# Windowed attention into a squared-ReLU FFN: spare slots and earlier visits for late pairs, and a last accumulator in two tiles

## The chip, the cores and the metric

The kernel runs on one core of a Trainium2 chip, in one launch. The metric is the device time of an execution in microseconds (us). The core's engines are TensorE (PE, matrix products), VectorE (DVE), ScalarE (ACT), GpSimd (POOL) and SyncE (SP, which here issues nearly all DMAs).

## The reference

Attention with 4 batches, 8 heads, 768 positions and a head dimension of 64. Each query sees the keys less than 16 positions away and, beside them, one summary for each of the 24 blocks of 32 positions (the largest of the block's keys by element, and the mean of its values). The result, 3072 tokens of 512 numbers, goes through a feed-forward network with 2048 hidden units and a squared ReLU.

```python
k_sum = k.reshape(B, H, nb, block, D).max(axis=3)
v_sum = v.reshape(B, H, nb, block, D).mean(axis=3)
scores_l_m = np.where(mask_l, scale * q @ k.T, -1e9)        # |i - j| < 16
scores_s = scale * np.einsum('bhsd,bhnd->bhsn', q, k_sum) + np.log(block)
a = softmax(np.concatenate([scores_l_m, scores_s], axis=-1))
x = (a @ np.concatenate([v, v_sum], axis=2)).reshape(3072, 512)
h = x @ w_in                  # 512 -> 2048
r = np.maximum(h, 0.0)
return (r * r) @ w_out        # 2048 -> 512
```

(The lines are shortened; the types are all 32-bit floats.)

## The kernel before, in words

**Numbers.** The feed-forward products are made of 32-bit floats that are split into a high and a low part, so that one product is three matmuls of 128x512 (high by high, high by low, low by high). An operand's high part is a cast on ACT (`gh`, L1810), its low part a subtraction on DVE (`gl`, L1815).

**Tiles.** The 3072 queries are 48 groups of 64, two of them a pair (24 pairs); eight groups (512 tokens) are a unit of the network, u = 0 to 5. Units 0 and 1 go through the network plainly. Units 2 to 5 go in two rounds, s = 0 (units 2 and 3) and s = 1 (units 4 and 5), each as two units by two halves of the network with seven block products instead of eight. The first products (`first_product`, L1492: `h` from `xh`, `xl` and a weight) make the hidden values; the second ones (`products`, L1738) are 56 chunks of six matmuls a round, numbered n = 0 to 55, into accumulators in PSUM of 128x1024 (`o_66`, `o_67`; each covers two banks, one for each half of 512 columns). `products(s, 0)` has the first 16 chunks, `products(s, 1)` the other 40. `copied` (ACT) and `plus` (DVE) bring an accumulator into SBUF or add it to what lies there, `leave` stores a finished block.

**Visits.** The attention of the later pairs is woven into the products. A visit on PE consists of the score matmuls of a pair n (Sn: `att` from keys `kb` and queries `q`, L734) and the value matmuls of an earlier pair v (Vv: `x` from the weights `a` and the values `v`, L1013); the table VISITS says which go together, and `visit_at` when each is due. Between the two lies `pair_softmax` (L890): DVE and ACT make the weights, DVE transposes them (L973), SP stores the transposed rows to memory (`turn`, L985, four DMAs) and fetches them back in another layout (`a`, L992, two DMAs of 384 and 128 KB). All pairs share one tile `a_81` for these rows, so that the fetch for one pair can start only when the value matmuls of the pair before have read theirs. Queries have two slots (`q`, loaded at L650), value rows three (`v_77` to `v_79`, one for each group, loaded at L671), weight chunks eight (loaded at L1794). `vps` (L606) are the matmuls of the block means of the last batch.

**Order.** A list scheduler, `Plan`, writes every engine's instructions in order before the launch. A task has an engine, an assumed cost, a key (when it is due), the tasks it comes after and the slots it takes and frees; of the tasks that are ready on an engine the one with the lowest key goes first. For a DMA the planner assumes a rate, a latency and what the argument `late` adds. On the chip each engine follows its list, and waits by semaphores where data or a slot are not there; SP too issues its DMAs in the list's order.

**The end.** The last chunk (n = 55 of s = 1) is emitted in two halves by columns, each of three matmuls. Both halves lie in one accumulator tile. The first half is copied by ACT (`copied`, L1752), the second by DVE (L1844), into two halves of one SBUF tile, and each is stored by a DMA (L1763).

## Time and profile before

| | us |
|---|---|
| median of three runs | 590.36 |
| lowest, highest | 589.26, 592.49 |
| the profiled execution | 593.21 |
| its span | 591.5 |
| PE busy in the span | 577.7 (98%) |
| PE load busy (weights, beside PE) | 469.1 (79%) |
| DVE busy | 413.6 (70%) |
| ACT busy | 353.7 (60%) |
| POOL busy | 69.5 (12%) |
| mean rate of the DMAs | 268 GB/s |

The span is the time from the first to the last instruction of the profiled execution; its own device time is 1.7 us longer. All starts below count from the span's beginning. The busy share of an engine is an average over the whole span; where the share is below one, the views by stretch tell where. The trace's visits can be told by their tiles: `att<-kb,q` are the scores, `x<-a,v` the values.

### The profile page before, as it was taken

The page shows a single profiled execution, that of the slowest core. Times are in us where ns is not written, and L with a number is a line of the kernel's source. Part 1 is how long each engine was busy: PE and PEld are TensorE (multiplying, and loading weights), DVE is VectorE, ACT ScalarE, POOL GpSimd, SP SyncE. Part 2 cuts the span into 40 slices and gives each one's busy share as a digit, 9 for nine tenths or more (in the row PEclk, how much of TensorE's full clock was granted, in tenths as well). Part 3 has the DMA queues.
Part 4 walks back from the last instruction along what each step waited for, and adds up shares of the span by engine and source line. Part 5 has one row for each costly group of instructions (what it writes and reads, how often), then busy time and mean ns, then how long its engine had stood idle before and what let it go on. Part 6 is the DMA issues. An engine that isn't in the chain of part 4 may idle for free.

```text
span 591.5 us, 12509 instructions
## 1 busy us (share of the span) xinstructions
PE 577.7 (98%) x4624; PEld 469.1 (79%) x4624; DVE 413.6 (70%) x652; ACT 353.7 (60%) x801; POOL 69.5 (12%) x116
## 2 busy tenths in 40 slices
PE   7989999999999999999999999999999999999996
PEld 6677887878888788878887788788887888788885
DVE  4899997864455578375877887689936533897653
ACT  1799876874663446456664556555556766755542
POOL 4500002214542820100000000000000000000000
PEclk9999999999999999999999999999999999999999
DMA  8996994689999759999999986988799785567672
GB/s 298 361 368 226 343 325 141 199 247 368 359 324 322 239 168 326 307 285 299 353 326 280 329 265 195 312 241 252 226 342 315 257 268 161 146 193 230 195 229 94
DMA packets 98474, 158.41 MB, mean 268 GB/s; under 512 B 9839, under 2 KB 54639, under 8 KB 98414
## 3 DMA queue, kind: packets, MB, share of 16 engines
q1 hardware_dynamic: 98030, 157.03, 81.7%
q8 instruction: 37, 0.61, 0.4%
q0 software_dynamic: 384, 0.59, 0.3%
q14 instruction: 23, 0.19, 0.1%
HBM read 112.16 MB, written 45.88 MB: 267 GB/s over the span
## 4 chain that ended last, share of the span: by engine, by line
PE 72%; DMA 11%; DVE 8%; SPq 3%; issue 2%; ACT 2%; DVEq 0%; ACTq 0%
PE o L1826 25%; PE h L1512 13%; PE o L1663 12%; PE o L1234 9%; PE h L1210 8%; PE x L1013 3%; DMA raw<-wW 3%; PE att L734 2%; DMA a<-turn 2%; DMA out<-os 2%; DMA v<-vF 1%; DVE w L1163 1%; DVE t L1155 1%; DMA fv_lent<-vS 1%; DVE raw L1149 1%
## 5 line engine op out<-in xcount | busy, mean ns | idle before, releaser
L1826 PE MATMUL o<-gh,w 128*128 128x512 f32 x448 | 121.1, 392 | 0.0
L1810 ACT CAST gh<-g 128x512 fp32r<-128x512 f32 x112 | 69.2, 621 | 56.0 <-PE o L1826 31.5
L1826 PEld LDWEIGHTS o<-gh,w 128*128 128x128 f32 x448 | 83.4, 188 | 18.0 <-issue 0.4
L1815 DVE TENSOR_TENSOR gl<-g,gh 128x512 fp32r<-128x512 f32 x112 | 75.5, 686 | 21.2 <-ACT gh L1810 21.0
L1210 PE MATMUL h<-xh,w 128*128 128x512 f32 x240 | 74.8, 393 | 0.1
L1512 PE MATMUL h<-xh,w 128*128 128x512 f32 x224 | 69.9, 393 | 0.2 <-DVE xl L1100 0.2
L1826 PE MATMUL o<-gl,w 128*128 128x512 f32 x224 | 69.2, 389 | 0.0
L1234 PE MATMUL o<-w,gh 128*128 128x512 f32 x240 | 61.9, 393 | 0.5 <-DVE w L1163 0.5
L935 ACT ACTIVATE p<-p,nm 128x88 f32<-128x88 f32 x120 | 42.7, 358 | 23.6 <-DVE nm L929 23.6
L1234 PEld LDWEIGHTS o<-w,gh 128*128 128x128 f32 x240 | 44.5, 188 | 10.6 <-DVE w L1163 0.9
L1210 PEld LDWEIGHTS h<-xh,w 128*128 128x128 f32 x240 | 44.6, 188 | 10.1 <-DVE xl L1100 0.6
L1512 PEld LDWEIGHTS h<-xh,w 128*128 128x128 f32 x224 | 41.6, 188 | 9.5 <-DVE xl L1100 0.6
L1826 PEld LDWEIGHTS o<-gl,w 128*128 128x128 f32 x224 | 42.0, 188 | 8.8
L1210 PE MATMUL h<-xl,w 128*128 128x512 f32 x120 | 46.7, 389 | 0.0
L1512 PE MATMUL h<-xl,w 128*128 128x512 f32 x112 | 43.6, 389 | 0.0
L1522 ACT ACTIVATE r<-h 128x512 f32<-128x512 f32 x32 | 19.1, 595 | 39.1 <-PE h L1512 36.0
L1224 DVE TENSOR_TENSOR gl<-r,gh 128x512 fp32r<-128x512 f32 x30 | 24.6, 823 | 15.0 <-ACT gh L1221 13.9
L1663 PE MATMUL o<-w,w 128*128 128x512 f32 x140 | 34.5, 390 | 0.0
L1234 PE MATMUL o<-w,gl 128*128 128x512 f32 x120 | 33.6, 389 | 0.0
L1803 DVE TENSOR_TENSOR g<-g 128x512 f32<-128x512 f32 x48 | 32.7, 687 | 1.0
L1219 ACT ACTIVATE r<-h 128x512 f32<-128x512 f32 x30 | 17.7, 591 | 23.5 <-PE h L1210 15.6
L1663 PEld LDWEIGHTS o<-w,w 128*128 128x128 f32 x140 | 26.2, 188 | 5.9 <-DVE u L1695 0.5
(198 smaller groups left out, 993.9 us busy)
## 6 DMA issues: line engine op xcount, KB each, us to landing
raw<-wW SPq DMA_DIRECT2D x32, 512.0 KB, 6.6
w<-scr_s SPq DMA_DIRECT2D x64, 256.0 KB, 3.0
w<-scr_a SPq DMA_DIRECT2D x48, 256.0 KB, 3.0
w<-scr_i SPq DMA_DIRECT2D x38, 256.0 KB, 5.1
scr_t<-ci SPq DMA_DIRECT2D x16, 512.0 KB, 5.4
turn<-ta SPq DMA_DIRECT2D x80, 96.0 KB, 3.8
a<-turn SPq DMA_DIRECT2D x20, 384.0 KB, 5.2
w<-scr_t SPq DMA_DIRECT2D x28, 256.0 KB, 3.6
```

The lines of the kernel that those rows point to most:

```text
L935: nc.scalar.activation(x, x, AF.Exp, bias=nm.tile[:, n : n + 1], accum_out=nm.tile[:, H + n : H + n + 1])
L1013: nc.tensor.matmul(x_of(i)[h % 2 * D : (h % 2 + 1) * D, h // 2, :], lhsT=v_bufs[g].tile[:rows, h * D : (h + 1) * D], rhs=av[:rows, 2 * c : ...
L1210: nc.tensor.matmul(cut(h), lhsT=lhs.tile[:, k * P : (k + 1) * P], rhs=rhs[:, k, c0 : c0 + n], start=(i == 0), stop=(i == 3 * KT - 1),)
L1224: lambda: nc.vector.tensor_tensor(out=cut(gl), in0=cut(r), in1=cut(gh).bitcast(F32), op=ALU.subtract),
L1234: nc.tensor.matmul(o_of(o, t), lhsT=terms[i][0].tile[:, (t - t0) * P : (t - t0 + 1) * P], rhs=terms[i][1].tile, start=(first and i == 0), ...
L1512: nc.tensor.matmul(h.tile, lhsT=lhs.tile[:, k * P : (k + 1) * P], rhs=rhs[:, k, c0 : c0 + TU], start=(i == 0), stop=(i == 3 * KT - 1),)
L1522: t2 = add(f"RL{name}", "ACT", 0.56, lambda: nc.scalar.activation(r.tile, h.tile, AF.Relu), due + 3, [t1], take=[r], use=[h])
L1663: nc.tensor.matmul(o.tile[:, bank], lhsT=chunk.tile[:, w * HALF + d * P : w * HALF + (d + 1) * P], rhs=xs[y][d], start=starts and i == 0, ...
L1803: lambda x=x, ins=ins, op=op: nc.vector.tensor_tensor(out=x.tile, in0=ins[0].tile, in1=ins[1].tile, op=op),
L1810: f"GH{s}_{n}", "ACT", 0.54, lambda x=x, gh=gh: nc.scalar.copy(out=gh.tile, in_=x.tile), due - 4, ready,
L1815: lambda x=x, gh=gh, gl=gl: nc.vector.tensor_tensor(out=gl.tile, in0=x.tile, in1=gh.tile.bitcast(F32), op=ALU.subtract),
L1826: nc.tensor.matmul(o.tile[:, d], lhsT=chunk.tile[:, w * HALF + d * P : w * HALF + (d + 1) * P], rhs=y.tile, start=begins and w == 0 and y ...
```

## The change

It has three parts. (1) Two pairs, 20 and 22, get their rows `a` in slots of the pool `t` (three tiles of 128x1024 which the second products use otherwise) and no more in the one tile `a_81`; and the planner assumes 2.5 us more for the fetch of `a` for pairs 12 and later (`late=TR_LATE`, in the planner only). (2) Seven visits (those with V17 to V23) are given earlier due times, by 8, 10 or 16 of the planner's us. (3) The accumulator that the last round's chunks of the first, third, fifth and seventh product share is two PSUM tiles of one bank each from the pool `h`, in place of one tile of two banks. `copied` and `plus` do two operations on it, one for each half; at the end DVE copies the first half and ACT the second, each into an SBUF tile of its own with a store of its own.

```diff
+SPARE_A = 20, 22
+TR_LATE = 2.5
+SOONER = {17: 8.0, 18: 8.0, 19: 10.0, 20: 16.0, 21: 16.0, 22: 16.0, 23: 16.0}
...
-        visit_at.append(at)
+        visit_at.append(at - SOONER.get(v, 0.0))
...
-                a_bufs[g] = buf("a", 1, (P, 2 * DM), F32, f"a{g}", fixed=True)
+                if g // 2 in SPARE_A:
+                    a_bufs[g] = buf("t", 3, (P, 2 * DM), F32, f"a{g}")
+                else:
+                    a_bufs[g] = buf("a", 1, (P, 2 * DM), F32, f"a{g}", fixed=True)
...
-        t_a = add(f"TR{g}", "SP", 0.8, fetch, fetch_at, [t_w], take=[a], use=[d], size=8 * P * DM, behind=last_of("turn", None))
+        t_a = add(f"TR{g}", "SP", 0.8, fetch, fetch_at, [t_w], take=[a], use=[d], size=8 * P * DM, behind=last_of("turn", None), late=TR_LATE if both[0] >= NW * 2 else 0.0)
...
+        if s == NS - 1:
+            if part == 0:
+                made["ends"] = tuple(h_buf(f"end{d}") for d in range(2))
+            acc[0] = made["ends"]
...
+        def halves(to, o):
+            if isinstance(o, tuple):
+                return [(by_two(to)[:, d], x.tile, d) for d, x in enumerate(o)]
+            return [(by_two(to), o.tile, slice(0, 2))]
...
+            def copy():
+                for x, y, _ in halves(to, o):
+                    nc.scalar.copy(out=x, in_=y)
...
+            def plus_():
+                for y, z, d in halves(to, o):
+                    nc.vector.tensor_tensor(out=y, in0=z, in1=by_two(x)[:, d], op=ALU.add)
...
-                            o.tile[:, d], lhsT=chunk.tile[:, w * HALF + d * P : w * HALF + (d + 1) * P], rhs=y.tile,
+                            o[d].tile if isinstance(o, tuple) else o.tile[:, d],
+                            lhsT=chunk.tile[:, w * HALF + d * P : w * HALF + (d + 1) * P], rhs=y.tile,
...
-                            t = copied("C21", tail, o, due + 2, [t_p], [tail], d)
-                        leave(f"21_{s}_{i}", tail, 1, 0, due + 3, [t], d)
+                        tail = buf("t", 3, (P, 2 * DM), F32, f"c21_{s}_{i}")
+                        copy = nc.scalar.copy if i else nc.vector.tensor_copy
+                        t = made["C21"] = add(
+                            f"C21_{s}_{i}", "ACT" if i else "DVE", 0.62, lambda copy=copy, x=o[i], to=tail: copy(out=to.tile[:, :TU], in_=x.tile),
+                            due + 2, [t_p], take=[tail], use=[o[i]],
+                        )
+                        rows = rest_out[HALF + i * P : HALF + (i + 1) * P, s * 2 * TU : s * 2 * TU + TU]
+                        add(
+                            f"PS21_{s}_{i}", "SP", 0.45, lambda rows=rows, tail=tail: nc.sync.dma_start(out=rows, in_=tail.tile[:, :TU]),
+                            due + 3, [t], use=[tail], size=4 * P * TU,
+                        )
```

How the lists move is seen best at three places. The first is on PE at S20 (the `att` rows; `gh_13` and `gl_13` are the operands of chunk n = 13). Before:

```order
680 L1826 MATMUL o_67<-gh_13_3756,w_986 128x512 x4
681 L1826 MATMUL o_67<-gl_13_3759,w_986 128x512 x2
682 L734 MATMUL att<-kb,q_3728 32x128 x16
683 L734 MATMUL att<-kb,q_3731 32x128 x16
684 L1826 MATMUL o_67<-gh_14_3768,w_868 128x512 x4
685 L1826 MATMUL o_67<-gl_14_3777,w_868 128x512 x2
686 L606 MATMUL vps_3835<-fv_0_3459,means 24x128 x8
687 L606 MATMUL vps_3835<-fv_2_3578,means 24x128 x8
688 L606 MATMUL vps_3835<-fv_4_3594,means 24x128 x8
689 L1826 MATMUL o_67<-gh_15_3779,w_868 128x512 x4
```

The same rows of the changed kernel:

```order
680 L1850 MATMUL o_67<-gh_13_3753,w_986 128x512 x4
681 L1850 MATMUL o_67<-gl_13_3758,w_986 128x512 x2
682 L1850 MATMUL o_67<-gh_14_3766,w_868 128x512 x4
683 L1850 MATMUL o_67<-gl_14_3769,w_868 128x512 x2
684 L740 MATMUL att<-kb,q_3739 32x128 x16
685 L740 MATMUL att<-kb,q_3742 32x128 x16
686 L612 MATMUL vps_3826<-fv_0_3459,means 24x128 x8
687 L612 MATMUL vps_3826<-fv_2_3578,means 24x128 x8
688 L612 MATMUL vps_3826<-fv_4_3594,means 24x128 x8
689 L1850 MATMUL o_67<-gh_15_3778,w_868 128x512 x4
```

S20 has gone one chunk back, behind n = 14, and `vps` follows it directly, where n = 14 stood between the two. Ahead of this place S19 with V15 has moved one chunk back too, from behind nine chunks to behind ten.

The second is on PE at V20 (`x<-a,v`). Before:

```order
833 L1826 MATMUL o_66<-gh_16_4459,w_932 128x512 x4
834 L1826 MATMUL o_66<-gl_16_4465,w_932 128x512 x2
835 L1826 MATMUL o_66<-gh_17_4469,w_932 128x512 x4
836 L1826 MATMUL o_66<-gl_17_4474,w_932 128x512 x2
837 L1826 MATMUL o_66<-gh_18_4472,w_986 128x512 x4
838 L1826 MATMUL o_66<-gl_18_4476,w_986 128x512 x2
839 L1826 MATMUL o_66<-gh_19_4504,w_986 128x512 x4
840 L1826 MATMUL o_66<-gl_19_4507,w_986 128x512 x2
841 L1013 MATMUL x_4524<-a_81,v_79 64x64 x8
842 L1013 MATMUL x_4524<-a_81,v_77 64x64 x8
843 L1826 MATMUL o_66<-gh_20_4510,w_868 128x512 x4
844 L1826 MATMUL o_66<-gl_20_4522,w_868 128x512 x2
```

In the changed kernel, at the same rows:

```order
833 L1850 MATMUL o_66<-gh_16_4461,w_932 128x512 x4
834 L1850 MATMUL o_66<-gl_16_4467,w_932 128x512 x2
835 L1019 MATMUL x_4492<-a_4346,v_79 64x64 x8
836 L1019 MATMUL x_4492<-a_4346,v_77 64x64 x8
```

V20 stands here behind n = 16. The rows that follow it, to V21:

```order
837 L1850 MATMUL o_66<-gh_17_4471,w_932 128x512 x4
838 L1850 MATMUL o_66<-gl_17_4474,w_932 128x512 x2
839 L1850 MATMUL o_66<-gh_18_4479,w_986 128x512 x4
840 L1850 MATMUL o_66<-gl_18_4489,w_986 128x512 x2
841 L1850 MATMUL o_66<-gh_19_4532,w_986 128x512 x4
842 L1850 MATMUL o_66<-gl_19_4536,w_986 128x512 x2
843 L1850 MATMUL o_66<-gh_20_4538,w_868 128x512 x4
844 L1850 MATMUL o_66<-gl_20_4549,w_868 128x512 x2
845 L1850 MATMUL o_66<-gh_21_4541,w_868 128x512 x4
846 L1850 MATMUL o_66<-gl_21_4551,w_868 128x512 x2
847 L1019 MATMUL x_4575<-a_81,v_78 64x64 x8
848 L1019 MATMUL x_4575<-a_81,v_79 64x64 x8
```

V20 has moved from behind n = 19 to behind n = 16 and reads a tile of its own, `a_4346`; V21 has moved from behind n = 30 to behind n = 21. In the same way V22 goes from behind n = 37 to behind n = 28, V23 from behind n = 41 to behind n = 36, V19 stands one hidden step (twelve matmuls of a first product) sooner, and V17 with S22 and V18 with S23 one such step later.

The third is SP's list, between the store of the transposed rows and the next loads. Before, from the value rows of pair 20's second group on (`v_77`; `v_78` holds those of pair 21's first group; `a_81<-turn_92` is pair 20's fetch, in two DMAs; the last row loads the value rows of pair 21's second group):

```order
293 L671 DMA v_77<-vS 96x512
294 L671 DMA v_78<-vS 96x512
295 L992 DMA a_81<-turn_92 96x1024
296 L992 DMA a_81<-turn_92 32x1024
297 L1794 DMA w_875<-scr_s_101 128x512
298 L1794 DMA w_875<-scr_s_102 128x512
299 L1363 DMA scr_i_118<-w_986 256x1x256
300 L1794 DMA w_932<-scr_s_95 128x512
301 L1794 DMA w_932<-scr_s_96 128x512
302 L1794 DMA w_986<-scr_s_97 128x512
303 L1794 DMA w_986<-scr_s_98 128x512
304 L671 DMA v_79<-vS 96x512
```

In the changed kernel pair 20's fetch stands directly behind pair 19's, further ahead:

```order
280 L677 DMA v_79<-vS 96x512
281 L998 DMA a_81<-turn_91 96x1024
282 L998 DMA a_81<-turn_91 32x1024
283 L998 DMA a_4346<-turn_92 96x1024
284 L998 DMA a_4346<-turn_92 32x1024
```

It stood at row 295 and is now at row 283. And the rows from the store of pair 23's transposed rows on, where `a_81<-turn_93` is pair 21's fetch, `a_4476<-turn_86` pair 22's, and the last row loads the value rows of pair 21's second group:

```order
293 L991 DMA turn_87<-ta_4421 32x3x256 x4
294 L1818 DMA w_868<-scr_s_99 128x512
295 L1818 DMA w_868<-scr_s_100 128x512
296 L998 DMA a_81<-turn_93 96x1024
297 L998 DMA a_81<-turn_93 32x1024
298 L998 DMA a_4476<-turn_86 96x1024
299 L998 DMA a_4476<-turn_86 32x1024
300 L1818 DMA w_875<-scr_s_101 128x512
301 L1818 DMA w_875<-scr_s_102 128x512
302 L1369 DMA scr_i_118<-w_986 256x1x256
303 L1818 DMA w_932<-scr_s_95 128x512
304 L677 DMA v_79<-vS 96x512
```

Pair 22's fetch stands directly behind pair 21's, and the load of the value rows of pair 21's second group is the eighth DMA behind the first one of pair 21's fetch. POOL's list is unchanged, and so is the order of the block products at the start of s = 1.

## Rows read from the trace of the kernel before

**Rows 1.** The page: its head line and the busy time of each engine (us, share of the span, instructions).

```profile
span 591.5 us, 12509 instructions
...
PE 577.7 (98%) x4624; PEld 469.1 (79%) x4624; DVE 413.6 (70%) x652; ACT 353.7 (60%) x801; POOL 69.5 (12%) x116
```

**Rows 2.** Busy time by stretch: the stretch and its length, then for each engine its busy us and, in brackets, its instructions; at the end the granted clock of TensorE as a share of full speed, the busy share of the DMA engines and the GB/s that they moved.

```profile
304.00:320.00 16.00, 15.52 (x253) 11.86 (x253) 11.47 (x17) 7.11 (x18) 0.00 (x0) 1.00 1.00 327
...
370.00:382.00 12.00, 10.68 (x74) 8.65 (x73) 8.06 (x13) 6.54 (x12) 0.00 (x0) 1.00 1.03 314
382.00:515.00 133.00, 132.95 (x662) 108.33 (x662) 86.18 (x138) 84.94 (x145) 0.00 (x0) 1.00 0.79 247
515.00:586.00 71.00, 71.00 (x315) 58.77 (x314) 51.37 (x76) 33.60 (x53) 0.00 (x0) 1.00 0.65 195
```

**Rows 3.** The waits of PE, the upper row in the stretch 304 to 320 us, the lower one in 370 to 382: engine, tile and line, what was waited for, us in total, times, longest.

```profile
PE att L734 <- DMA q<-qW: 0.4, 1, 0.4
...
PE x L1013 <- DMA a<-turn: 1.3, 1, 1.3
```

**Rows 4.** Timeline of the end, all engines (585 to 592 us): start, us, engine (SPq is SP's queue, which issues the DMAs), line, operation, out<-in, form and count; in brackets how long the engine had been idle and what ended that.

```profile
585.74 0.39 PE L1826 MATMUL o<-gl,w 128*128 128x512 f32 x1
...
586.42 0.39 PE L1826 MATMUL o<-gl,w 128*128 128x512 f32 x1
586.85 0.59 ACT L1752 COPY c<-o 128x512 f32<-128x512 f32 x1 [3.91 <-PE o L1826]
587.46 1.06 SPq L1763 DMA_DIRECT2D out<-c  x2
587.47 0.69 DVE L1844 COPY c<-o 128x512 f32<-128x512 f32 x1 [3.80 <-ACT c L1752]
```

**Rows 5.** Timeline of PE around visits S19 (the first two rows) and S20, 303 to 321 us, columns as before. A row is a run of equal matmuls; its length holds the modelled end of the last one, so that rows overlap.

```profile
304.06 0.61 PE L1826 MATMUL o<-gl,w 128*128 128x512 f32 x2
...
305.69 1.15 PE L1013 MATMUL x<-a,v 128*64 128x64 f32 x32
...
311.02 1.07 PE L1826 MATMUL o<-gh,w 128*128 128x512 f32 x4
...
312.38 1.07 PE L1826 MATMUL o<-gh,w 128*128 128x512 f32 x4
313.29 0.61 PE L1826 MATMUL o<-gl,w 128*128 128x512 f32 x2
...
315.65 1.19 PE L1826 MATMUL o<-gh,w 128*128 128x512 f32 x4
...
317.25 1.51 PE L606 MATMUL vps<-fv,means 128*24 128x128 f32 x48
```

**Rows 6.** The chain that ended last: start, us, what. A DMA's row is from its issue to its landing.

```profile
232.94 2.72 PE h L1512 x12
...
311.07 3.94 DMA q<-qW
...
353.51 1.08 PE x L1013 x32
...
368.46 1.11 PE x L1013 x32
...
372.45 6.66 DMA a<-turn
```

**Rows 7.** Timeline of PE around visits V20 and V21, 375 to 397 us.

```profile
377.31 0.61 PE L1826 MATMUL o<-gl,w 128*128 128x512 f32 x2
379.25 1.15 PE L1013 MATMUL x<-a,v 128*64 128x64 f32 x32 [1.32 <-DMA a<-turn]
380.33 1.20 PE L1826 MATMUL o<-gh,w 128*128 128x512 f32 x4
...
394.96 0.61 PE L1826 MATMUL o<-gl,w 128*128 128x512 f32 x2
...
396.59 0.73 PE L1826 MATMUL o<-gh,w 128*128 128x512 f32 x2
```

**Rows 8.** The DMAs of three stretches: 355 to 357 us (the first two rows), 369 to 386 us (the next three; the first of them is what all DMA engines moved) and 379.9 to 381 us (the last). An issue's row has its count, KB each, and the median us from issue to landing.

```profile
v<-vS SPq DMA_DIRECT2D x2, 192.0 KB, 2.6
a<-turn SPq DMA_DIRECT2D x1, 384.0 KB, 5.2
...
DMA packets 2737, 5.19 MB, mean 305 GB/s; under 512 B 338, under 2 KB 845, under 8 KB 2735
...
v<-vS SPq DMA_DIRECT2D x4, 192.0 KB, 4.8
a<-turn SPq DMA_DIRECT2D x2, 384.0 KB, 6.8
...
v<-vS SPq DMA_DIRECT2D x2, 192.0 KB, 5.4
```

**Rows 9.** The waits of SP's queue, 375 to 380 us.

```profile
SPq L1794 <- DMA a<-turn: 1.8, 1, 1.8
```

**Rows 10.** Timeline of SP's queue, at the store of pair 23's transposed rows.

```profile
366.67 1.83 SPq L985 DMA_DIRECT2D turn<-ta  x4
```

**Rows 11.** The instructions of line 1752 (ns: shortest, median, longest; start of the first and the last; form).

```profile
L1752 ACT COPY u<-o x6: 1007/1011/1016, 303.4 to 554.3; 128x1024 f32<-128x1024 f32 x6
```

**Rows 12.** The page's groups of instructions: busy us and mean ns of one, then the idle time of the engine before them and what ended most of it.

```profile
L1810 ACT CAST gh<-g 128x512 fp32r<-128x512 f32 x112 | 69.2, 621 | 56.0 <-PE o L1826 31.5
```

More of the change, by code (lines that the diff above doesn't have):

```diff
@@ L1745, in products, with all_of, copied @@
         *acc, u2, u5, made = sums[s]
+        if s == NS - 1:
+            if part == 0:
+                made["ends"] = tuple(h_buf(f"end{d}") for d in range(2))
+            acc[0] = made["ends"]
         bank = acc[0], acc[1], acc[0], acc[2], acc[0], acc[2], acc[0]
         after = []
-        def copied(name, to, o, key, deps, take=(), d=slice(0, 2)):
+        def halves(to, o):
+            if isinstance(o, tuple):
+                return [(by_two(to)[:, d], x.tile, d) for d, x in enumerate(o)]
+            return [(by_two(to), o.tile, slice(0, 2))]
+        def all_of(o):
+            return list(o) if isinstance(o, tuple) else [o]
+        def copied(name, to, o, key, deps, take=()):
+            def copy():
+                for x, y, _ in halves(to, o):
+                    nc.scalar.copy(out=x, in_=y)
             made[name] = add(
-                f"{name}_{s}_{d.start}", "ACT", 0.09 + 0.44 * (d.stop - d.start),
-                lambda: nc.scalar.copy(out=by_two(to)[:, d], in_=o.tile[:, d]), key, deps, take=take, use=[o] + [to] * (not take),
+                f"{name}_{s}", "ACT", 0.97 + 0.09 * isinstance(o, tuple), copy, key, deps, take=take, use=all_of(o) + [to] * (not take)
             )
@@ L1765, in leave, with plus @@
             )
-        def plus(name, to, o, x, key, deps, take=(), d=slice(0, 2)):
+        def plus(name, to, o, x, key, deps, take=()):
+            def plus_():
+                for y, z, d in halves(to, o):
+                    nc.vector.tensor_tensor(out=y, in0=z, in1=by_two(x)[:, d], op=ALU.add)
             made[name] = add(
-                f"{name}_{s}_{d.start}", "DVE", 0.13 + 0.56 * (d.stop - d.start),
-                lambda: nc.vector.tensor_tensor(out=by_two(to)[:, d], in0=o.tile[:, d], in1=by_two(x)[:, d], op=ALU.add),
-                key, deps, take=take, use=[o, x] + [to] * (not take),
+                f"{name}_{s}", "DVE", 1.25 + 0.1 * isinstance(o, tuple), plus_, key, deps, take=take,
+                use=[*all_of(o), x] + [to] * (not take),
             )
@@ L1833, in products @@
                         f"FP{s}_{n}_{i}", "PE", 0.2268 * len(piece), lambda piece=piece, mm=mm: mm(piece), due + 0.1 * i,
-                        [t_h, t_l, t_c] + after, take=[o] * begins, use=[chunk, gh, gl] + [o] * (not begins),
+                        [t_h, t_l, t_c] + after, take=all_of(o) * begins, use=[chunk, gh, gl] + all_of(o) * (not begins),
                         behind=last_of("product", None),
@@ L1838, in products @@
                     if end:
-                        d = slice(i, i + 1)
-                        if not i:
-                            tail = buf("t", 3, (P, 2 * DM), F32, f"c21_{s}")
-                        if i:
-                            t = made["C21"] = add(
-                                f"C21_{s}_{i}", "DVE", 0.62, lambda: nc.vector.tensor_copy(out=by_two(tail)[:, 1:], in_=o.tile[:, 1:]),
-                                due + 2, [t_p], use=[o, tail],
-                            )
-                        else:
-                            t = copied("C21", tail, o, due + 2, [t_p], [tail], d)
-                        leave(f"21_{s}_{i}", tail, 1, 0, due + 3, [t], d)
+                        tail = buf("t", 3, (P, 2 * DM), F32, f"c21_{s}_{i}")
[9 more added lines that the diff above has]
+                        )
                 after = []
```

## The prediction

> **What bounds the kernel now.** I read the page's head first: TensorE (PE) is busy for 577.7 of a span of 591.5 us, 98% [rows 1]. So the time is set by PE's own work, which the change leaves as it is (same products, same visits, same block means), and by the few microseconds in which PE stands still. The second view, busy time by stretch, says where these are: 15.52 of 16 us are busy from 304 to 320, 10.68 of 12 from 370 to 382, and nothing is missing from 382 to 515 (0.05 us) and from 515 to 586 (0.00) [rows 2]. Third, what PE waited for in the two stretches with holes: a DMA that brings `q` (0.4 us, once) and a DMA that brings `a` from `turn` (1.3 us, once) [rows 3]. The timeline of PE shows both places, and the end of the span shows a third: PE is done at 586.81, and then two copies follow one another, on ACT and on DVE, before the last store is issued [rows 4]. The change touches these three places; everything else is PE's order.
>
> **First place, visit S20 (scores of pair 20).** An undisturbed entry into a visit is S19's: from the start of the last `gl` matmuls at 304.06 to what follows the 64 score matmuls at 305.69 is 1.63 us. S20's is 313.29 to 315.65, 2.36 us [rows 5]. The difference, 0.73 us, is the wait: 0.4 before the block [rows 3], and the rest inside it, since the second group's `q` lands at 311.07 + 3.94 = 315.01 [rows 6], while the block's second half was due at about 313.29 + 0.54 + 0.55 = 314.4. After the change one more product stands ahead of S20 in all (ten before S19, five between V15 and S20); an ordinary product goes from 311.02 to 312.38, 1.36 us [rows 5]. S20 then starts at 313.29 + 0.54 + 1.36 = 315.2 and its second half 0.55 us later, at 315.74. One load of a weight chunk is now issued ahead of `q`; at 0.4 us a load the `q` lands by 315.4. So the 0.73 us go, with 0.3 us to spare. If the load comes later than that, the wait returns in the part that it is late; taken: gain 0.73, bounds 0 and 0.73.
>
> **The switch behind it.** Before, a product stands between S20 and the block means (`vps`): 315.65 to 317.25 is 1.60 us, against 1.36 for one among its like [rows 5]. The extra 0.24 us is what PE pays for going from one kind of work to another and back. Now `vps` follows S20 directly and this product stands among its like. Gain 0.24, bounds 0 (the change of kind between S20 and `vps` costs as much) and 0.24.
>
> **Second place, visit V20 (values of pair 20).** An undisturbed entry is V21's: 394.96 to 396.59, 1.63 us. V20's is 377.31 to 380.33, 3.02 us [rows 7]. The difference is 1.39 us. Its cause in the chain of waits: the fetch of pair 20's rows is issued at 372.45 and lands 6.66 us later [rows 6]. It could not go earlier, since all pairs share one slot `a`, and V19 (368.46 + 1.11 = 369.57) must have read pair 19's rows first [rows 6]. After the change pair 20 has a slot of its own, and its fetch stands in SP's queue right behind pair 19's, which waits for V18. V18 ends at 353.51 + 1.08 = 354.59 [rows 6], and in the new order it stands one step of the first product (2.72 us [rows 6]) later, less the 0.97 us gained by then: 356.3. The issues of two fetches, 0.9 us each, follow, and 6.8 us, the longest latency of that stretch [rows 8], bring pair 20's rows by 365. V20 itself moves three products sooner: products 16 to 19 fill about 372.4 to 377.85 (four of 1.36 us), all of that 0.97 us sooner, so V20 is due at 371.4 + 1.36 + 0.04 = 372.8. Margin: 7 us. The `v` rows of pair 20 wait for V19's end (now near 365.8), and land within 6 us of it, 1 us ahead of V20. So 1.39 us go. Bounds: 0, if a slot `t` or the queue of SP keeps the fetch late, and 1.39.
>
> **What is late next: V21.** It moves much further, nine products sooner, and stands now five products behind V20: 373.9 + 5 x 1.36 + 0.2 = 380.9 us. Its second group's `v` load takes the slot that V20 frees at 373.9, and in SP's order it is the eighth DMA behind the first half of pair 21's fetch. An issue of SP waits for the DMA eight before it: the trace has such a wait, of 1.8 us, of a chunk load for a fetch `a<-turn` [rows 9], and in the order shown for SP these two are eight apart. The fetch of pair 21 is issued when pair 23's transposed rows are stored, which begins at 366.67 now and lasts 1.83 us [rows 10], and two chunk loads (0.4 us each) are issued: 369.6, or up to 370.5 if the softmax of pair 23 follows its later scores. With 5.2 to 6.8 us to landing [rows 8] it lands at 375 to 377.3. The `v` load behind it takes between 2.6 us (the quiet stretch) and 5.4 us (the full one) [rows 8], and no more than a fetch's 6.8. It lands between 377.6 and 384.1, and PE's wait at V21 is between 0 and 3.2 us. I take the rows of this stretch: landing of the fetch 376.8, and 4.8 us more, 381.6: a wait of 0.7 us, new.
>
> Here the trace and a rule can be weighed. From 369 to 386 the mean rate is 305 GB/s [rows 8]. From the second half of pair 21's fetch to that `v` load SP hands out 128 + 384 + 128 + 4 x 256 + 192 KB = 1.90 MB, 6.2 us at this rate. Were they served in the order of their issues, the load would land that much behind the fetch's first half, at 381.2 to 383.5; the 381.6 taken is near the early end, since two rates run side by side in these queues (4.8 us for a small load, 6.8 for a large one). The Trainium skill ("DMA: Bandwidth & Descriptors", Specifications) gives about 358 GB/s as the limit of one core's traffic with the memory; by it the 1.90 MB are an estimated 5.3 us, the load would land 0.9 us sooner, V21 would not wait, and the sum would be 0.7 us better. The trace's mean of this stretch, 305, stays under that figure, so the row is kept.
>
> V22 and V23 move sooner too (nine and five products). Pair 22's fetch goes to a slot of its own behind pair 21's; pair 23's waits for V21. Between V22 at about 391 and V23 at about 403 stand eight products (10.9 us), more than one fetch (6.8) and one `v` load (5.4 us) in parallel. I cost them at nothing; the cover gone, each would cost up to 2 us.
>
> **Third place, the end.** The last product's first half ends at 585.74 + 0.39 = 586.13, the second at 586.81. ACT copies the first half from 586.85 for 0.59 us although it was there 0.7 us before: both halves are one tile `o`. DVE waits for ACT (3.80 us idle, put down to it), begins at 587.47, ends at 588.16 [rows 4]. Now each half is a tile. DVE can begin at 586.15 (ends 586.84), ACT at 586.85 (ends 587.44). The last store is issued 588.16 - 587.44 = 0.72 us sooner. Gain 0.72; bounds 0 (the stores 0.6 us apart get in each other's way, or a wait on the whole stays) and 0.9.
>
> **What it adds.** U1 and U2 become two ACT copies each: 2 x 0.59 [rows 4] in place of 1.01 us [rows 11], so 0.17 us more, and C22 two additions, about as much more. PE's busy time is full from 382 to 586 but for 0.05 us [rows 2], so it waits for none of them now; ACT itself idles 31.5 us for PE's products [rows 12]. Cost 0. The two `h` tiles that the accumulator takes have no other user once the first products are done. If one of these copies held PE's next product back, it would be 0.17 us.
>
> **Sum.** 0.73 + 0.24 + 1.39 + 0.72 - 0.7 = 2.4 us. The profiled execution took 593.21 us (span 591.5 and 1.7 around it) and would take 590.8. The median shown is 590.36, 2.85 us under the profiled one; the gains lie in waits that recur in every execution, so I take them off the median: 588.0.
>
> **Rivals.**
> A, as summed: 588.0.
> B, V21 does not wait, because its fetch is out by 369.6 and lands in the 5.2 us of the quieter row: 590.36 - 3.1 = 587.3. For it: S23 and pair 23's softmax run beside a DVE with gaps; against it: the full queues from 369 on.
> C, one of the gains does not come. Either V20 keeps its wait, because the spare slot or SP's order holds the fetch (only 0.73 + 0.24 + 0.72 = 1.7 us are left, of which the 0.7 at V21 go off: 589.4), or the end gives nothing, and 2.4 - 0.7 = 1.7 leaves 588.7. For it: the queue of SP is in order and its waits (1.8 us) are PE's next holes; against it: 7 us of margin at V20.
> D, slower: V21 becomes the bound by more than was gained. Place: the `v` load of pair 21's second group, stuck behind the fetch by the rule of eight. Landing of the fetch at 377.8 (7.3 us, longer than any row, since two fetches now stand together) and 6.8 us for the load give 384.6, a wait of 3.7 us, 0.6 us more than all gains: 591.0. It decides from a landing at 380.9 + 3.1 = 384.0 on. For it: the two fetches of 512 KB are issued together; against it: no `v` load in these rows took over 5.4 us.
>
> **How the numbers follow.** A 0.42, B 0.24, C 0.22, D 0.08, and 0.04 for something unseen. The predicted time is A's. The range runs from 586.3 (B, with 1 us that a median of three runs, 589.26 to 592.49, can be off) to 590.8 (D's near side). What a measurement of this kernel can tell from no change is about 0.5%, 2.95 us: faster means under 587.41, slower over 593.31. Of A about a quarter, of B rather more than half fall under 587.41, terms and scatter together (0.11 + 0.14, and 0.02 of the rest): faster 0.27. Slower needs D doubled: 0.06. The rest, 0.67, is within it.
>
> **What would show it.** In the changed kernel's trace: no wait of PE for `q` from 304 to 320 and the visit S20 in 1.63 us with `vps` at its heels; no wait at V20; a wait of 0 to 3.2 us of V21 for `v` (not for `a`), near 381; busy time of 382 to 515 as full as now; DVE's copy ahead of ACT's at the end and 0.6 to 0.7 us between PE's last matmul and the last issue, against 1.4 now. Wrong would be a wait at V22 or V23, a wait of ACT's `gh` that lets PE stand still behind a visit, or V20 still waiting for `a<-turn`.

## The result and the profile after

The changed kernel took 593.89 us (median of five runs, 593.09 to 595.51) against 590.36 us before (589.26 to 592.49, five runs too): a ratio of 1.0059, with a 95% interval of 1.0032 to 1.0086. It is slower by 3.5 us, and the forecast was 588.0 with a range up to 590.8. The same kernel timed again on another occasion, twelve runs beside 24 of before, gave 593.81 against 592.85 us, a ratio of 1.0011 (0.9991 to 1.0030). So the loss is clear of noise on the first occasion alone; on the second the median is 1.0 us higher and the interval holds no change as well. On neither was there a gain. Part of what moves the size is told below: a stretch at half the clock, which some executions have and others have not.

The profiled execution of the changed kernel took 595.51 us. Its page begins with these rows (to be read beside [rows 1]):

```profile
span 593.8 us, 12512 instructions
...
PE 578.8 (97%) x4624; PEld 470.3 (79%) x4624; DVE 415.8 (70%) x653; ACT 353.2 (59%) x803; POOL 70.0 (12%) x116
```

The span is 2.3 us longer, and PE is busy 1.1 us longer with the same number of instructions. By stretch, with the columns of [rows 2], and one row for a short stretch behind V21:

```profile
304.00:320.00 16.00, 14.99 (x252) 11.76 (x251) 11.79 (x17) 6.02 (x14) 0.00 (x0) 1.00 0.93 315
...
370.00:382.00 12.00, 12.00 (x83) 9.54 (x83) 8.43 (x14) 7.24 (x13) 0.00 (x0) 1.00 0.93 284
382.00:515.00 133.00, 130.36 (x644) 106.47 (x643) 82.35 (x132) 81.97 (x140) 0.00 (x0) 0.99 0.79 242
515.00:586.00 71.00, 71.00 (x315) 58.62 (x314) 53.55 (x82) 36.32 (x60) 0.00 (x0) 1.00 0.68 203
385.40:388.80 3.40, 3.40 (x21) 2.71 (x18) 1.29 (x2) 1.20 (x2) 0.00 (x0) 0.50 1.08 339
```

Three things are to be seen. From 370 to 382 PE is full: the hole at V20 is closed. From 382 to 515, where 0.05 us were missing, 2.64 us are missing now. And from 385.4 to 388.8 the granted clock is 0.50, the lower of TensorE's two levels (1.2 GHz). From 304 to 320 there is more idle time than before (1.01 us against 0.48), not less. What PE waited for, over the whole execution, in the columns of [rows 3]:

```profile
PE x L1019 <- DMA v<-vS: 2.6, 1, 2.6
...
PE o L1850 <- DMA w<-scr_a: 1.0, 1, 1.0
...
PE att L740 <- DMA q<-qW: 0.7, 1, 0.7
```

The first row is V21, the second is the chunk of weights for product n = 9. The third lies at 204 us, ahead of everything that the change moves; waits of up to 1.3 us ahead of 300 us come and go between the profiles of all these kernels.

The first place, in the columns of [rows 5]:

```profile
303.74 0.61 PE L1850 MATMUL o<-gl,w 128*128 128x512 f32 x2
305.37 1.17 PE L1850 MATMUL o<-gh,w 128*128 128x512 f32 x4 [1.01 <-DMA w<-scr_a]
...
306.93 1.16 PE L740 MATMUL att<-kb,q 64*32 64x128 f32 x64
...
315.58 0.61 PE L1850 MATMUL o<-gl,w 128*128 128x512 f32 x2
316.12 1.16 PE L740 MATMUL att<-kb,q 64*32 64x128 f32 x64
317.21 1.51 PE L612 MATMUL vps<-fv,means 128*24 128x128 f32 x48
```

S20 goes as forecast: 315.58 to 317.21 is 1.63 us, and `vps` follows directly. But ahead of S19 stands a wait of 1.01 us for a chunk of weights, `scr_a`. That row is product n = 9, which the changed order puts ahead of S19 and V15.

The second place, in the columns of [rows 7]:

```profile
373.19 0.61 PE L1850 MATMUL o<-gl,w 128*128 128x512 f32 x2
373.74 1.15 PE L1019 MATMUL x<-a,v 128*64 128x64 f32 x32
374.82 1.19 PE L1850 MATMUL o<-gh,w 128*128 128x512 f32 x4
...
381.30 0.61 PE L1850 MATMUL o<-gl,w 128*128 128x512 f32 x2
381.84 0.69 PE L1019 MATMUL x<-a,v 128*64 128x64 f32 x16
385.12 0.93 PE L1019 MATMUL x<-a,v 128*64 128x64 f32 x16 [2.60 <-DMA v<-vS]
385.98 2.08 PE L1850 MATMUL o<-gh,w 128*128 128x512 f32 x4
...
388.71 1.13 PE L1850 MATMUL o<-gh,w 128*128 128x512 f32 x4
...
390.12 1.07 PE L1850 MATMUL o<-gh,w 128*128 128x512 f32 x4
```

V20 (373.74) does not wait. V21 begins at 381.84, does its first group, and stands still for 2.60 us until the second group's values are there. From the last `gl` matmuls ahead of it to the product behind it are 381.30 to 385.98, 4.68 us, where an undisturbed visit takes 1.63: 3.05 us lost. About 0.25 of them are already the lower clock, since the second group up to the next product takes 0.86 us (385.12 to 385.98), and 0.61 us at full clock in the repetition below (384.06 to 384.67). The product behind it takes 385.98 to 388.71, 2.73 us; the next takes 388.71 to 390.12, 1.41 us.

SP's queue in that stretch (`v<-vS` at 378.62 loads the values of pair 21's second group and one more):

```profile
371.50 1.36 SPq L1818 DMA_DIRECT2D w<-scr_s  x2
372.96 1.78 SPq L998 DMA_DIRECT2D a<-turn  x4
...
378.62 0.84 SPq L677 DMA_DIRECT2D v<-vS  x2
```

its wait ahead of that load:

```profile
SPq L677 <- DMA a<-turn: 1.7, 1, 1.7
```

and the load itself in the chain that ended last:

```profile
378.62 6.46 DMA v<-vS
```

The end, in the columns of [rows 4]:

```profile
588.64 0.39 PE L1850 MATMUL end<-gl,w 128*128 128x512 f32 x1
...
589.06 0.69 DVE L1867 COPY c<-end 128x512 f32<-128x512 f32 x1 [2.50 <-PE end L1850]
...
589.32 0.39 PE L1850 MATMUL end<-gl,w 128*128 128x512 f32 x1
589.74 0.59 ACT L1867 COPY c<-end 128x512 f32<-128x512 f32 x1 [3.91 <-PE end L1850]
```

DVE copies the first half while PE is at the second, ACT the second half directly behind PE. From the start of the last matmuls to the end of the span are 593.8 - 589.32 = 4.48 us, where it was 591.5 - 586.42 = 5.08: 0.60 us won.

**The account of the two profiled executions.** PE's last matmuls start at 589.32 instead of 586.42, 2.90 us later. Up to the end of n = 8 the changed kernel is 0.32 us ahead (303.74 against 304.06 [rows 5]); this is scatter of the early part, where the order is the same. It then loses about 1.3 at n = 9 (303.74 to 306.93 is 3.19 us, where one product and the way into a visit take 1.36 + 0.54) and wins about 1.0 back at S20 and `vps`, so that it leaves this place almost level; wins 1.39 at V20; loses 3.05 at V21 and 1.3 at half clock behind it (2.73 - 1.5, the length that this product has behind a visit at full clock in the repetition below, and 0.05 of the next one). The sum is +2.9; with 0.6 back at the end, 2.3 us, the difference of the spans. The medians of the first occasion differ by 3.5 us; the 1.2 us beyond have no place in these two profiles.

### The profile page after: what moved, and what is told of

Its sections match the earlier page's. It is cut to its first block, busy times and chain, and to the rows that moved or that the text cites. A ratio compares the mean times of both kernels' runs of the same rounds, so it can differ in the third digit from the quotient of the medians.

```text
span 593.8 us, 12512 instructions
## 1 busy us (share of the span) xinstructions
PE 578.8 (97%) x4624; PEld 470.3 (79%) x4624; DVE 415.8 (70%) x653; ACT 353.2 (59%) x803; POOL 70.0 (12%) x116
## 4 chain that ended last, share of the span: by engine, by line
PE 71%; DMA 11%; DVE 9%; ACT 3%; SPq 3%; issue 2%; DVEq 0%; ACTq 0%
PE o L1850 17%; PE h L1518 15%; PE o L1669 12%; PE o L1240 8%; PE end L1850 7%; PE h L1216 6%; DMA raw<-wW 3%; PE x L1019 3%; PE att L740 2%; DVE t L1161 2%; DVE w L1169 2%; ACT p L941 1%; DVE raw L1155 1%; DMA v<-vF 1%; DMA qvpa_lent<-vF 1%
## 5 line engine op out<-in xcount | busy, mean ns | idle before, releaser
L1850 PE MATMUL o<-gh,w 128*128 128x512 f32 x320 | 87.4, 395 | 1.0 <-DMA w<-scr_a 1.0
L1850 PEld LDWEIGHTS o<-gh,w 128*128 128x128 f32 x320 | 60.1, 190 | 14.2 <-ACT gh L1834 1.4
L1850 PE MATMUL o<-gl,w 128*128 128x512 f32 x160 | 49.7, 392 | 0.0
L1850 PEld LDWEIGHTS o<-gl,w 128*128 128x128 f32 x160 | 30.3, 189 | 6.4
L1850 PE MATMUL end<-gh,w 128*128 128x512 f32 x128 | 34.5, 390 | 0.0
## 6 DMA issues: line engine op xcount, KB each, us to landing
a<-turn SPq DMA_DIRECT2D x20, 384.0 KB, 5.4
```

Source lines behind the costliest of these rows:

```text
L1850: nc.tensor.matmul(o[d].tile if isinstance(o, tuple) else o.tile[:, d], lhsT=chunk.tile[:, w * HALF + d * P : w * HALF + (d + 1) * P], rhs ...
```

## Experiments

Theory T: the gains are there in about the forecast size, and the loss is made by three things that the prediction sized too small or left out, V21's wait, the half clock behind it, and the chunk of n = 9. The rivals are named where they are tested. All ratios are against the kernel before, timed beside each on the same chip; its medians there were 592.55 us for the first four experiments, 592.85 for the next four, 592.48 for the last two.

**e1: the end alone.**

```diff
-SPARE_A = 20, 22
-TR_LATE = 2.5
-SOONER = {17: 8.0, 18: 8.0, 19: 10.0, 20: 16.0, 21: 16.0, 22: 16.0, 23: 16.0}
+SPARE_A = ()
+TR_LATE = 0.0
+SOONER = {}
```

> Only the end of the change (two PSUM tiles, two engines at once); the order of every visit is as before. Theory T (the loss is V21's wait of 3.05 us, 1.4 us of half clock behind it and 1.1 us of wait for the weights of chunk n = 9, against gains of 2.4 us at S20, vps and V20 and 0.6 us at the end): 0.6 us below the kernel before, no wait of PE behind 382 us. Rival R1 (the two tiles, with more and smaller copies, hold PE back): 2 us or more above before.

Measured: 591.59 us, ratio 0.9986 (0.9970 to 1.0002), 0.96 us less than before, with the interval just touching no change, so that the profile and not the time shows this gain. R1 falls: there is nothing slower in it, and PE is as full as before behind 382 us. Its timeline at the end shows the two copies as in the changed kernel, the second one started 0.04 us behind PE's last matmul (584.82 + 0.39):

```profile
584.82 0.39 PE L1850 MATMUL end<-gl,w 128*128 128x512 f32 x1
585.25 0.59 ACT L1867 COPY c<-end 128x512 f32<-128x512 f32 x1 [3.91 <-PE end L1850]
```

**e2: V21 three products later.**

```diff
-SOONER = {17: 8.0, 18: 8.0, 19: 10.0, 20: 16.0, 21: 16.0, 22: 16.0, 23: 16.0}
+SOONER = {17: 8.0, 18: 8.0, 19: 10.0, 20: 16.0, 21: 8.0, 22: 16.0, 23: 16.0}
```

> The whole change, but V21 is made due 8 of the planner's units sooner, not 16: it stands behind n = 24, three products (4.1 us) later, V23 one product sooner; the fetches of pairs 20 to 22 are handed out as in the changed kernel. Theory T: V21 is due at 386.5 on that profile's scale, its values land at 385.1, so no wait and no half clock: 593.9 - 4.4 = 589.5. Rival R2 (SP's queue is late altogether, so that the next visits wait in V21's place): a wait of 2 us or more at V22 or V23, and 592 or more. Rival R1: no change from 593.9.

Measured: 590.09 us, ratio 0.9956 (0.9940 to 0.9972). V21's row:

```profile
385.21 1.15 PE L1019 MATMUL x<-a,v 128*64 128x64 f32 x32
```

The visit goes through in one run, and PE has no wait at V22 or V23 (124.96 of 125 us busy from 390 to 515). R2 and R1 fall: moving this one visit turns the loss into a gain of 2.5 us.

**e3: the change without its end.** The functions of the second products are those of before, all else is as in the changed kernel.

```diff
-            acc[0] = made["ends"]
...
-                        copy = nc.scalar.copy if i else nc.vector.tensor_copy
...
+                            t = copied("C21", tail, o, due + 2, [t_p], [tail], d)
+                        leave(f"21_{s}_{i}", tail, 1, 0, due + 3, [t], d)
```

> The whole change without its end (one accumulator tile, the copies of before). Theory T: 0.6 us above the changed kernel, 594.5. Rival R1: back to 591 or below.

Measured: 593.81 us, ratio 1.0017 (0.9998 to 1.0037), the same median as the changed kernel's repetition; R1 falls here too. The difference of the end, 0.6 us, can't be told apart from these runs. V21 waits again, and the product behind it is slow again (2.08 us for its four `gh` matmuls, where the rows at full clock have 1.2):

```profile
383.34 0.81 PE L1019 MATMUL x<-a,v 128*64 128x64 f32 x16 [2.17 <-DMA v<-vS]
384.07 2.08 PE L1832 MATMUL o<-gh,w 128*128 128x512 f32 x4
```

**e4: the first place as before.**

```diff
-late=TR_LATE if both[0] >= NW * 2 else 0.0
+late=TR_LATE if both[0] >= 32 else 0.0
```

> The whole change, but the planner's 2.5 us more are assumed for pairs 16 and later, not 12: S19 stands behind nine products again, S20 behind n = 13 and vps behind n = 14, as before; V17 to V23 as in the changed kernel, and pair 21's fetch is handed out two chunk loads sooner. Theory T: no wait of PE for the chunk of n = 9 (1.1 us back), S20's wait for q and the switch are there again (0.97 us lost), V21 waits 2 to 3 us for v: 593 to 594. Rival R3 (the wait at n = 9 is scatter of the DMAs and comes in any order): it is as likely here as in the changed kernel, and the time is 594.5 or more.

Measured: 594.48 us, ratio 1.0021 (1.0002 to 1.0040). The time lies above T's 593 to 594 and about where R3 has it; what speaks against R3 is the profile alone. There is no wait for n = 9 in it, S20 waits for `q` again (0.4 us), and V21 waits for `v`:

```profile
383.52 0.69 PE L1019 MATMUL x<-a,v 128*64 128x64 f32 x16 [2.70 <-DMA v<-vS]
384.13 1.21 PE L1850 MATMUL o<-gh,w 128*128 128x512 f32 x4
```

The wait is as long as in the changed kernel, and yet the product behind it runs at full clock here. The chain shows the load: it is issued at 376.00, when the first half of pair 21's fetch had long landed (374.07), and takes 7.47 us:

```profile
376.00 7.47 DMA v<-vS
```

The eighth DMA ahead of it is a chunk load in this order, and held it less (`L677` are the loads of `v`, two of them):

```profile
SPq L677 <- DMA w<-scr_s: 1.2, 2, 0.6
```

From V20's end, which frees the slot, to the issue are 2.9 us (373.11 to 376.00), where the changed kernel has 3.8 (374.82 to 378.62); from V20's end to the landing are 10.4 us here and 10.3 us there. What the shorter hold gave, the load lost on its way through the queues.

**e5: the changed kernel again.** No edit.

> The changed kernel itself, beside the others on one chip. Theory T: 1 to 3.5 us above before; executions in which PE runs at half clock behind V21's wait (mean granted clock 0.997 or less) are 2 to 3 us longer than those at 0.999 or more, and the rest is within 1 us of before.

Measured: 593.81 us (590.86 to 595.38), ratio 1.0011 (0.9991 to 1.0030). The mean granted clock of an execution was 0.997 or less in eight of twelve, with a median of 594.11 us, and 1.000 in four, with a median of 591.88 us, below the 592.85 of before. The profiled execution is one of the four. Its rows at n = 9 and at V21:

```profile
304.95 1.17 PE L1850 MATMUL o<-gh,w 128*128 128x512 f32 x4 [1.14 <-DMA w<-scr_a]
...
384.06 0.69 PE L1019 MATMUL x<-a,v 128*64 128x64 f32 x16 [1.95 <-DMA v<-vS]
384.67 1.20 PE L1850 MATMUL o<-gh,w 128*128 128x512 f32 x4
```

Both waits are there, 1.14 and 1.95 us, and behind V21 the clock is full. The wait for n = 9 comes in the same place as in the first profile.

**e6: one spare slot, V21 in the same place.**

```diff
-SPARE_A = 20, 22
-SOONER = {17: 8.0, 18: 8.0, 19: 10.0, 20: 16.0, 21: 16.0, 22: 16.0, 23: 16.0}
+SPARE_A = 20,
+SOONER = {17: 8.0, 18: 8.0, 19: 10.0, 20: 16.0, 21: 12.0, 22: 16.0, 23: 16.0}
```

> The changed kernel with a spare slot for pair 20 alone, and V21 made due 12 units sooner, so that V19 to V21 stand at the same products as in the changed kernel. Pair 22's fetch (512 KB) no longer stands between pair 21's fetch and the load of pair 21's second group of values, which is the sixth DMA behind the fetch's first half and not the eighth. Theory T (the load is late through the fetches in front of it: by the wait for the eighth before it, and by their bytes): V21's wait falls from 2.2 to 2.7 us to 1 us or less, 2 to 3 us are won against the changed kernel. Rival R4 (the load is late because the slot comes free with V20's end, whatever stands in front): V21 waits 2 us or more as before, and the time is the changed kernel's.

Measured: 589.89 us, ratio 0.9950 (0.9932 to 0.9968), none of seven executions under a clock of 0.999. V21 and what follows it:

```profile
381.78 1.41 PE L1019 MATMUL x<-a,v 128*64 128x64 f32 x32
383.12 1.20 PE L1850 MATMUL o<-gh,w 128*128 128x512 f32 x4
```

The visit is one run of 1.34 us to the next product, 0.25 more than its like. In SP's queue the two issues are

```profile
373.28 0.84 SPq L998 DMA_DIRECT2D a<-turn  x2
...
376.38 0.96 SPq L677 DMA_DIRECT2D v<-vS  x2
```

The fetch goes out as late as in the changed kernel, and lands at 378.15; the value load goes out at 376.38, 1.8 us ahead of that landing, where in the changed kernel it went out 0.07 us behind it (378.62 against 378.55). It takes 6.08 us. R4 falls: V20's end is at the same place and the load goes out 2.2 us sooner and lands 2.6 us sooner. So pair 22's fetch in front of it is what made it late. Whether by the hold of the DMA eight places ahead or by its 512 KB is not parted here, since both go together; e4, where a shorter hold alone gave nothing, says that the bytes count too. The 3.9 us won against the changed kernel (593.81) are more than T's 2 to 3.

**e7: V21 one product later.**

```diff
-SOONER = {17: 8.0, 18: 8.0, 19: 10.0, 20: 16.0, 21: 16.0, 22: 16.0, 23: 16.0}
+SOONER = {17: 8.0, 18: 8.0, 19: 10.0, 20: 16.0, 21: 11.0, 22: 16.0, 23: 16.0}
```

> The changed kernel with V21 one product (1.36 us) later, behind n = 22; the fetches of pairs 20 to 22 as there. Theory T: the wait falls to 0.8 to 1.4 us, the half clock is rarer or gone, and 1.4 to 2.8 us are won against the changed kernel. Rival R2 (the values are late by the same amount wherever V21 stands): the wait stays over 2 us.

Measured: 590.82 us, ratio 0.9966 (0.9949 to 0.9982), one of twelve executions at a clock under 0.998. Product n = 9 and V21's second group:

```profile
303.85 1.17 PE L1850 MATMUL o<-gh,w 128*128 128x512 f32 x4 [1.22 <-DMA w<-scr_a]
...
382.72 0.69 PE L1019 MATMUL x<-a,v 128*64 128x64 f32 x16 [0.49 <-DMA v<-vS]
```

One product, 1.36 us of work, is worth 3.0 us of median against the changed kernel (593.81), since the wait shrinks from about 2 to 0.5 us and low mean clocks are nearly gone. T had 0.8 to 1.4 us of wait and 1.4 to 2.8 us won, both missed on the good side. R2 falls once more. The wait at n = 9 stands, 1.22 us.

**e8: the mended version.** V21 later, S19 back behind n = 8, S20 left behind n = 14.

```diff
-SOONER = {17: 8.0, 18: 8.0, 19: 10.0, 20: 16.0, 21: 16.0, 22: 16.0, 23: 16.0}
+SOONER = {17: 8.0, 18: 8.0, 19: 10.0, 20: 16.0, 21: 8.0, 22: 16.0, 23: 16.0}
...
+        at += 2 * (n == 20)
         visit_at.append(at - SOONER.get(v, 0.0))
...
-late=TR_LATE if both[0] >= NW * 2 else 0.0
+late=TR_LATE if both[0] >= 32 else 0.0
```

> V21 three products later as in e2, S19 back behind nine products (the 2.5 us more for pairs 16 and later only), but S20 still behind n = 14 with vps at its heels. Theory T: no wait for the chunk of n = 9 and none at V21; of S20's wait at most 0.4 us; 0.5 to 1 us less than e2, 3 us less than before. Rival R3 (the wait at n = 9 is scatter): the same as e2 within 0.3 us, and a wait for w before S19 or behind it in this profile too.

Measured: 589.07 us (588.00 to 590.42), ratio 0.9939 (0.9920 to 0.9958): 3.8 us less than before and the lowest ratio of all. It was not timed beside e2, and the intervals of the two ratios overlap, so the times do not show that it gains on e2. All places of the change are full in its profile:

```profile
304.00:320.00 16.00, 16.00 (x196) 12.82 (x191) 11.77 (x18) 7.61 (x26) 0.00 (x0) 1.00 0.95 302
...
370.00:382.00 12.00, 12.00 (x81) 9.80 (x80) 8.46 (x13) 6.83 (x12) 0.00 (x0) 1.00 1.02 300
382.00:390.00 8.00, 8.00 (x71) 6.26 (x71) 7.93 (x14) 4.65 (x8) 0.00 (x0) 1.00 1.01 321
```

R3 would have kept a wait for n = 9; there is none.

**e9: without the planner's lateness.**

```diff
-TR_LATE = 2.5
+TR_LATE = 0.0
```

> The changed kernel without the planner's 2.5 us more for late fetches. S19, S20 and vps stand as before; V19 stands behind the second hidden step of its unit ahead, V20 behind n = 16, V21 behind n = 18, three products sooner than in the changed kernel; its second group's value load stands behind eleven chunk loads. Theory T (V21 set too early for its values is what costs, and the half clock follows a long wait): V21 waits 4 us or more, nearly all executions have a mean granted clock of 0.997 or less, and the time is 2 us or more above the changed kernel, 595.5 or more. Rival R5 (the planner's lateness itself makes the loss): no wait at V21 and 591 or less.

Measured: 595.44 us, ratio 1.0045 (1.0027 to 1.0064). R5 falls: the lateness in the planner is not the loss, it holds the visits back a little. But T's wait of 4 us or more was too much: the profile has 2.5 us at V21, with the half clock behind it, and waits that the changed kernel's profile has not (0.9 us at S20 for `q`, 0.9 at V17 for a fetch, 0.8 at V19 for ACT's `r`):

```profile
382.74 0.91 PE L1019 MATMUL x<-a,v 128*64 128x64 f32 x16 [2.53 <-DMA v<-vS]
383.57 2.08 PE L1850 MATMUL o<-gh,w 128*128 128x512 f32 x4
```

Seven of twelve executions had a mean clock of 0.997 or less, not nearly all.

**e10: spare slots and the end only.**

```diff
-TR_LATE = 2.5
-SOONER = {17: 8.0, 18: 8.0, 19: 10.0, 20: 16.0, 21: 16.0, 22: 16.0, 23: 16.0}
+TR_LATE = 0.0
+SOONER = {}
```

> Only the two spare slots and the end; no visit is made due sooner and no lateness assumed. S19 to vps stand as before, V20 behind n = 18 (one product sooner), V21 behind n = 30 and V22 behind n = 37 as before, V23 behind n = 39. Theory T: V20's wait of 1.4 us is gone, since its fetch goes out behind pair 19's, the end gives 0.6, S20's wait for q stays: 2.0 us below before. Rival R6 (V20 then waits for its values, which need V19's end, nearly as long): 0.6 to 1 us below before.

Measured: 591.11 us, ratio 0.9978 (0.9962 to 0.9993), 1.4 us less than before: between T (2.0) and R6 (0.6 to 1), so the medians do not part the two. The profile does:

```profile
370.00:382.00 12.00, 12.00 (x81) 9.78 (x80) 8.61 (x14) 7.20 (x13) 0.00 (x0) 1.00 1.02 288
```

V20's hole is closed without any visit's due time being lowered. In this execution S20 did not wait either.

## Why the prediction was wrong, point by point

**The step that failed is V21's wait, with two costs beside it that were put at nothing.** The prediction priced the wait at 0.7 us, and named 3.2 as its end. It was 2.60 us in the profile, 3.05 with what is lost within the visit. Two terms of it were too small. The fetch of pair 21 was to be issued at 369.6 to 370.5 and to land at 376.8; it was issued at 372.96 and landed at 378.55, since the stores of pair 23's rows began 2 us later than before (368.71, not 366.67 [rows 10]) and took 2.31 us, and the two chunk loads between had a wait of their own. And the value load took 6.46 us, not the 4.8 of the row that was chosen; in the profiles of e2 to e9 it took 5.8 to 7.5 us, always more than the 5.4 of the fullest row, once more than the 6.8 that was to be the end. So the values landed at 385.08, not 381.6. That the wait was no longer is due to PE: V21 began at 381.84, not 380.9, and its second group is needed only behind the first, 0.6 us later, which the prediction did not count. The place and the hold were right: the load waited for the first half of pair 21's fetch, the eighth DMA ahead of it. The trace shows that wait (1.7 us) and the issue 0.07 us behind the landing, and in the profiles of e2, e3, e5, e7 and e8 the issue is 0.06 to 0.07 us behind that landing too. The hold is not the whole of it, as e4 shows: with less of it the values came as late.

With 3.05 in the place of 0.7 the forecast's own sum gives 590.36 - 3.08 + 3.05 = 590.3, still inside its range. The loss needed two costs that the sum put at nothing, 1.3 us each; with them the sum is 592.9.

**What had no term: the half clock.** Behind the long wait, PE ran at 0.50 of its clock for 3.4 us, which cost 1.3 us behind the visit and about 0.25 within it. The prediction's rival D had the right place and the right kind of price: a loss from a landing at 384.0 on, 591.0 with a wait of 3.7 us. The load landed behind that limit, and with this term a wait of 2.6 us was enough. Rival D was given a chance of 0.08, and even its time, 591.0, was too low.

**What else had no term: n = 9.** The prediction counted what a later S19 gives S20, and not that product n = 9 now stands where S19 stood, 2.17 us sooner, while its chunk comes when it came before. The chunk's load was issued at 299.19, between queries, values and a fetch, and took 6.04 us. In the three profiles in which PE's wait there is put down to the chunk (1.01, 1.14, 1.22 us), and two more in which it is put down to ACT's `gh` (0.8 and 0.9 us, e3 and e6), S19 stands behind n = 9 (in e2, of the same order, 0.3 us are lost there); in the profiles with S19 behind n = 8 there is no wait ahead of S19. This loss, about 1.3 us in the profile, takes back what S20 and `vps` give. It is read from the profiles; no difference of times here shows it by itself.

**First place.** S20's wait went in the profile of the change, as forecast, and the visit took 1.63 us. It is not a sure gain: with the same order the wait for `q` was 0.4 us in e3 and e6. The switch: `vps` behind S20 costs no more than in its old place (317.21 to 318.65, 1.44 us, the row that follows being a product at its usual length). The two terms, 0.97 us, were right in kind; n = 9 cancels them, and the mended version has this stretch full, without that wait.

**Second place.** The 1.39 us at V20 came in full: 373.19 to 374.82 was 1.63 us and the stretch from 370 to 382 is full. 

**The end.** 0.60 us in the profile against a term of 0.72; the end alone gave 0.96 us in the medians, with an interval that holds both, and no change. The extra copies cost nothing: 71.00 of 71 us are busy from 515 to 586, and R1 fell twice.

**The rule on bandwidth.** The prediction weighed the Trainium skill ("DMA: Bandwidth & Descriptors", Specifications), which gives about 358 GB/s for one core, against 305 GB/s. By the rule V21 would not have waited; it waited. Nor did the row on rates, 305 GB/s, give the landing. From the issue of the second half of pair 21's fetch to the landing of that load (373.38 to 385.08) the trace has

```profile
DMA packets 1738, 3.39 MB, mean 290 GB/s; under 512 B 211, under 2 KB 482, under 8 KB 1737
```

The rate is near the one taken, but 3.39 MB were moved and not the 1.90 MB that the prediction counted: transfers from before and behind ran in the same 11.7 us.

**What stays open.** Why one execution has the half clock and another has not is not settled. A stretch of 3.4 us at 0.50 takes 0.003 off an execution's mean clock, which is 0.997 in the profile of the change, so the mean is taken here as its sign. It goes with V21's wait: 31 of 53 timed executions of the five kernels in which V21 waits for 1.9 to 2.7 us (the change twice, without its end, first place as before, without lateness) had a mean clock of 0.997 or less, and 3 of 57 of the six others. But a wait of 2.17 us had it and one of 2.70 us had not, so the length of that one wait does not decide alone. Nor was it tried to bring V21's values earlier with V21 left in place and both spare slots kept, or to part the hold of the eighth DMA from the bytes in front. Why before stood at 590.36 us on the first occasion and at 592.5 to 592.9 later is not known; only ratios within an occasion were compared.

## What to carry to other kernels

When work is pulled forward on a full engine, every operand of the work that takes its place, and of the work that is pulled, has a new deadline: list them all, those of the neighbours too, and look for each one's load in the queue with what it queues behind. Price a load in a full stretch by the longest latency that a row of that stretch has for any load of its size or larger, and not by the median; even that, 6.8 us, was passed once here (7.47). A wait that is removed at one visit is worth nothing if the next visit is moved up into a longer one; here one product of distance, 1.36 us, was worth 3 us.

## What was not expected of the hardware

A wait of 2 to 3 us in the midst of 577 us of steady matmuls was followed, in about half of the executions (by their mean clock), by a granted clock of 0.50 for some 3.4 us. Three profiles have it, with waits of 2.60, 2.17 and 2.53 us (the change, without its end, without lateness): from 385.4 to 388.8, 383.7 to 387.2 and 383.0 to 386.4, each time from 0.3 to 0.4 us after PE had gone on. Two have waits of 1.95 and 2.70 us and full clock behind them. The executions that had a low mean clock were 2.2 to 3 us longer by their medians (594.11 against 591.88 in the repetition, 594.62 against 591.66 without the end, 595.33 against 592.61 with the first place as before). The stretch itself costs about 1.5 us in the profile, 1.3 of them behind the visit; the rest is longer waits in the same executions, or something that no profile here shows. V20's wait of 1.32 us in the kernel before [rows 7] was followed by products at full clock.
